# Turning softmax products and dense rows by transposing DMAs instead of TensorE, with layer 1's columns first

## The chip, the cores and the metric

The kernel runs on one core of a Trainium2 chip. The core has five engines with queues of their own: TensorE (PE, matmuls, with a separate lane PEld for loading weights), VectorE (DVE), ScalarE (ACT), GpSimd (POOL) and SyncE (SP, which computes nothing and issues DMAs). Sixteen DMA engines move data between HBM, SBUF and SBUF. The metric is the device time of one execution in microseconds (us).

## The reference

Four blocks follow each other: memory-augmented attention, a dense ReLU layer, and both again with the same weights. All tensors are bf16 outside.

```python
x = x + A(layernorm(x), mem0)      # layer 0
x = x + B(layernorm(x))
x = x + A(layernorm(x), mem0)      # layer 1
x = x + B(layernorm(x))            # x: [1, 2048, 512]

def A(x, mem):                     # 64 segments of 32 rows, 8 memory rows, 32 heads of 128
    for s in range(64):
        h = concat([mem, x[32*s:32*s+32]])          # 40 rows
        q, k, v = h @ Wq, h @ Wk, h @ Wv            # per head
        p = softmax(mask(q @ k.T * 128**-0.5))      # 40 x 40 per head
        o = (p @ v) @ Wo                            # 40 x 512
        mem, out[s] = o[:8], o[8:]                  # the memory goes into the next segment

def B(x): return relu(x @ w1) @ w2                  # 512 -> 1376 -> 512
```

The segments of one layer depend on each other through the eight memory rows: segment s + 1 cannot begin its queries, keys and values before segment s has its whole output projection.

## The kernel before

**Two layers at once.** A step k does segment k of layer 0 and segment k - 4 (`DELTA`) of layer 1 together. There are 68 steps; the first four and the last four have one layer alone. The two segments lie side by side as 80 columns (2 x `L`, L = 40) of a tile `HT` (two of them, used in turn), with the model dimension on the partitions: layer 0's 32 rows and 8 memory rows, then layer 1's 8 memory rows and 32 rows. All projections are matmuls with a 128 x 128 block of weights as the stationary operand and these 80 columns moving.

**A step.** `prep_x` (POOL) copies the next 32 normalised columns of each layer into `HT`. `step_values` makes the values of 64 columns (all that depend on the memory, and what else fits in 64); the other 16 rows of layer 0 are taken from values made ahead of time (`late_values`, `early_values`) and are brought from HBM by `place_values`, which also places the others: four DMAs V<-vw and two V<-vh per step on SP. Then five units follow (`UNITS`; units 0 to 2 have eight heads, units 3 and 4 four):

- `queries_keys`: Q and K of four heads at a time, 16 matmuls each, into one of five PSUM banks `work`; ACT or DVE copies them to `qT`, `kT`.
- `scores`: 40 x 40 products, half-width tiles (64 columns of the array), then the softmax in rows on DVE and ACT: mask (L1093), maximum (L1097), subtract (L1100), exp on ACT (L1104), sum (L1107), reciprocal (L1110), product (L1124) into `P`, with heads on partition halves and key columns along the row.
- still in `scores`: `P` is turned on TensorE, by a matmul with a unit matrix `ident` as the moving operand (`turn`, L665 through the helper `across`), into another `work` bank. Two copies (`keep`, L1147 on ACT or L1149 on DVE) multiply it by 1 or 0 by partition half (`half`), and so make a block-diagonal operand `PT` of two heads.
- `attend`: values times `PT` (L1166), copied to `OT`.

`project` multiplies `OT` by Wo for all heads into the bank `st`, and copies eight columns to the next `HT` (the memory) and 64 to `OX` (the rows). After every second step `finish_pair` takes two segments of each layer: it turns `OX` back into rows on TensorE (`turn`), adds x, and runs the dense layer: `layernorm` (statistics on DVE, the power on POOL), a turn of the normalised rows `xr` on TensorE with a copy to `xnM`, w1, ReLU, w2. Its rows for layer 0 are normalised again and turned into `xnB`, layer 1's input.

**Order.** The kernel is written out by hand ahead of the build. A planner (`Plan`) knows every operation with an assumed cost and its dependencies by tiles and keys, simulates six queues and gives each engine its order; `PLACE`, `AHEAD` and `RULE` are tables of due times that shift operations in it, and `PAIRED` names projections that may run as two half-width matmuls instead of one whole. The array loses time when it changes between whole (128 columns) and half-width (64) tiles, so the planner prefers to stay in a kind. Each engine then works through its own order and waits only on semaphores; the planner's costs decide the order and nothing else at run time. SP's order is fixed in the same way: a DMA whose data isn't ready holds up those behind it.

Buffers that matter here: five `work` banks, `qT` and `kT` of four tiles each, `es` two, `PT` three, and one `P` tile per unit pair (`Pt`), whose unused columns are zeroed once.

Of the kernel before, what the change touches and what calls it, by code (L numbers as in the profile page):

```python
# [10 lines left out]
ALU = mybir.AluOpType  # L11
# [19 lines left out]
RULE = (0.0676, 338.0438, 3554579.0286, 1242705613.0663)  # L31
PERIOD = 42.8582
PLACE = {
    ("attend.mmu0.0", 0): 608.991, ("attend.mmu0.0", 1): 157.899, ("attend.mmu0.0", 2): -380.976,
    ("attend.mmu0.0", 3): -849.744, ("attend.mmu0.0", 4): -420.014, ("attend.mmu0.0", 5): 379.888,
    ("attend.mmu0.0", 6): -935.369, ("attend.mmu1.0", 0): 724.653, ("attend.mmu1.0", 1): 735.673,
    ("attend.mmu1.0", 2): 83.429, ("attend.mmu1.0", 3): -335.179, ("attend.mmu1.0", 4): 3.094,
    ("attend.mmu1.0", 5): -935.256, ("attend.mmu1.0", 6): -23.81, ("attend.mmu2.0", 0): -313.198,
    ("attend.mmu2.0", 1): -1055.43, ("attend.mmu2.0", 2): 351.452, ("attend.mmu2.0", 3): -29.526,
    ("attend.mmu2.0", 4): -812.532, ("attend.mmu2.0", 5): 234.539, ("attend.mmu2.0", 6): -65.699,  # L40
    ("attend.mmu3.0", 0): 13.451, ("attend.mmu3.0", 1): 157.484, ("attend.mmu3.0", 2): 133.291,
    ("attend.mmu3.0", 3): -203.514, ("attend.mmu3.0", 4): 192.222, ("attend.mmu3.0", 5): -84.323,
    ("attend.mmu3.0", 6): -139.89, ("attend.mmu4.0", 0): -853.255, ("attend.mmu4.0", 1): -244.026,
    ("attend.mmu4.0", 2): -305.761, ("attend.mmu4.0", 3): -104.638, ("attend.mmu4.0", 4): -89.602,
    ("attend.mmu4.0", 5): -204.344, ("attend.mmu4.0", 6): 50.714, ("dense_layer.mm.0", 1): 822.894,
    ("dense_layer.mm.0", 3): 717.325, ("dense_layer.mm.0", 6): 792.485, ("dense_layer.mm.1", 1): -268.282,
    ("dense_layer.mm.1", 3): 157.778, ("dense_layer.mm.1", 6): -380.794, ("dense_layer.mm.2", 1): 376.492,
    ("dense_layer.mm.2", 3): 130.965, ("dense_layer.mm.2", 6): -212.381, ("dense_layer.mm.3", 1): -70.602,
    ("dense_layer.mm.3", 3): 419.403, ("dense_layer.mm.3", 6): -774.382, ("dense_layer.mm.4", 1): -244.79,
    ("dense_layer.mm.4", 3): 367.889, ("dense_layer.mm.4", 6): -182.649, ("dense_layer.mm.5", 1): 943.633,  # L50
    ("dense_layer.mm.5", 3): -26.387, ("dense_layer.mm.5", 6): 595.003, ("finish_pair.turn.0", 1): -125.119,
    ("finish_pair.turn.0", 3): -175.437, ("finish_pair.turn.0", 6): -732.778, ("g0", 2): -902.623,
    ("g1", 2): -345.827, ("g2", 2): 376.933, ("g3", 2): -860.996, ("g4", 2): 261.098, ("g5", 2): -902.521,
    ("g6", 2): 262.286, ("g7", 2): 447.122, ("late_values.mmv0.0", 0): 7.391, ("late_values.mmv1.0", 0): 723.22,
    ("late_values.mmv2.0", 0): -33.087, ("late_values.mmv3.0", 0): -918.158, ("late_values.mmv4.0", 0): 711.016,
    ("late_values.mmv5.0", 0): -29.506, ("late_values.mmv6.0", 0): -417.119, ("late_values.mmv7.0", 0): -388.807,
    ("layernorm.turn.0", 1): -11.687, ("layernorm.turn.0", 3): 291.45, ("layernorm.turn.0", 6): 74.607,
    ("layernorm.turn.1", 1): 932.83, ("layernorm.turn.1", 3): -23.815, ("layernorm.turnr.0", 0): 130.977,
    ("layernorm.turnr.1", 0): 22.148, ("prepare.turns.0", 2): 138.08, ("project.mm.0", 0): -28.38,
    ("project.mm.0", 1): -813.549, ("project.mm.0", 2): -352.721, ("project.mm.0", 3): 338.425,  # L60
    ("project.mm.0", 4): -85.099, ("project.mm.0", 5): 395.603, ("project.mm.0", 6): 258.346,
    ("project.mm.1", 0): 382.886, ("project.mm.1", 1): 332.847, ("project.mm.1", 2): -815.345,
    ("project.mm.1", 3): 420.621, ("project.mm.1", 4): -904.087, ("project.mm.1", 5): 539.837,
    ("project.mm.1", 6): 66.403, ("project.mm.2", 0): 332.311, ("project.mm.2", 1): -807.177,
    ("project.mm.2", 2): -643.677, ("project.mm.2", 3): 169.374, ("project.mm.2", 4): 38.108,
    ("project.mm.2", 5): 154.46, ("project.mm.2", 6): -123.487, ("project.mm.3", 0): -94.659,
    ("project.mm.3", 1): -2.385, ("project.mm.3", 2): -392.671, ("project.mm.3", 3): 755.857,
    ("project.mm.3", 4): 239.419, ("project.mm.3", 5): 449.254, ("project.mm.3", 6): 237.48,
    ("project.mm.4", 0): -28.331, ("project.mm.4", 1): -89.329, ("project.mm.4", 2): 233.897,
    ("project.mm.4", 3): -897.55, ("project.mm.4", 4): 4.166, ("project.mm.4", 5): -271.575,  # L70
    ("project.mm.4", 6): 68.861, ("queries_keys.mmu0.0", 0): -114.972, ("queries_keys.mmu0.0", 1): -803.223,
    ("queries_keys.mmu0.0", 2): 449.473, ("queries_keys.mmu0.0", 3): -814.936, ("queries_keys.mmu0.0", 4): 64.492,
    ("queries_keys.mmu0.0", 5): -247.66, ("queries_keys.mmu0.0", 6): -321.229, ("queries_keys.mmu0.1", 0): -246.448,
    ("queries_keys.mmu0.1", 1): -83.345, ("queries_keys.mmu0.1", 2): -93.12, ("queries_keys.mmu0.1", 3): -67.094,
    ("queries_keys.mmu0.1", 4): -882.377, ("queries_keys.mmu0.1", 5): -142.63, ("queries_keys.mmu0.1", 6): -836.169,
    ("queries_keys.mmu0.2", 0): -921.465, ("queries_keys.mmu0.2", 1): -331.089, ("queries_keys.mmu0.2", 2): -36.099,
    ("queries_keys.mmu0.2", 3): -153.588, ("queries_keys.mmu0.2", 4): 0.628, ("queries_keys.mmu0.2", 5): -845.834,
    ("queries_keys.mmu0.2", 6): -937.81, ("queries_keys.mmu0.3", 0): -75.904, ("queries_keys.mmu0.3", 1): -26.436,
    ("queries_keys.mmu0.3", 2): -78.722, ("queries_keys.mmu0.3", 3): -83.815, ("queries_keys.mmu0.3", 4): -874.602,
    ("queries_keys.mmu0.3", 5): -285.858, ("queries_keys.mmu0.3", 6): -288.873,  # L80
    ("queries_keys.mmu1.0", 0): -287.689, ("queries_keys.mmu1.0", 1): -807.17, ("queries_keys.mmu1.0", 2): 138.905,
    ("queries_keys.mmu1.0", 3): -775.344, ("queries_keys.mmu1.0", 4): 333.755, ("queries_keys.mmu1.0", 5): -69.094,
    ("queries_keys.mmu1.0", 6): -299.934, ("queries_keys.mmu1.1", 0): -894.335,
    ("queries_keys.mmu1.1", 1): -300.828, ("queries_keys.mmu1.1", 2): -195.096,
    ("queries_keys.mmu1.1", 3): -407.541, ("queries_keys.mmu1.1", 4): -99.416, ("queries_keys.mmu1.1", 5): -928.29,
    ("queries_keys.mmu1.1", 6): -1007.777, ("queries_keys.mmu1.2", 0): -397.855,
    ("queries_keys.mmu1.2", 1): -271.199, ("queries_keys.mmu1.2", 2): -95.574, ("queries_keys.mmu1.2", 3): -424.872,
    ("queries_keys.mmu1.2", 4): -828.244, ("queries_keys.mmu1.2", 5): -84.504, ("queries_keys.mmu1.2", 6): -365.113,
    ("queries_keys.mmu1.3", 0): -267.974, ("queries_keys.mmu1.3", 1): -319.862, ("queries_keys.mmu1.3", 2): 11.67,
    ("queries_keys.mmu1.3", 3): -410.531, ("queries_keys.mmu1.3", 4): 44.01, ("queries_keys.mmu1.3", 5): -391.768,  # L90
    ("queries_keys.mmu1.3", 6): -213.718, ("queries_keys.mmu2.0", 0): -65.556, ("queries_keys.mmu2.0", 1): -240.632,
    ("queries_keys.mmu2.0", 2): 64.693, ("queries_keys.mmu2.0", 3): 448.514, ("queries_keys.mmu2.0", 4): 417.76,
    ("queries_keys.mmu2.0", 5): 347.423, ("queries_keys.mmu2.0", 6): -104.214, ("queries_keys.mmu2.1", 0): -34.178,
    ("queries_keys.mmu2.1", 1): 23.812, ("queries_keys.mmu2.1", 2): -196.254, ("queries_keys.mmu2.1", 3): -337.37,
    ("queries_keys.mmu2.1", 4): 139.933, ("queries_keys.mmu2.1", 5): -92.169, ("queries_keys.mmu2.1", 6): 434.453,
    ("queries_keys.mmu2.2", 0): 129.446, ("queries_keys.mmu2.2", 1): 68.117, ("queries_keys.mmu2.2", 2): -78.718,
    ("queries_keys.mmu2.2", 3): -0.671, ("queries_keys.mmu2.2", 4): 460.034, ("queries_keys.mmu2.2", 5): 252.252,
# [103 lines left out]


def t_dve(n, rate=1):
    return 0.065 + 1.042e-3 * n / rate


PART, MASKED = {ACT: 0.13, DVE: 0.10}, {ACT: 0.11, DVE: 0.065}


def t_pool(n):  # L210
    return 0.06 + 2.2e-3 * n


# [204 lines left out]
def kernel(  # L418
# [529 lines left out]
    def htx(i, a):  # L948
        return [("HTx", i, a, (0, X1)[a])]
# [383 lines left out]
```

## Time and profile before

| | |
|---|---|
| times of the runs shown | 1629.60 and 1625.38 us, median 1627.49 |
| profiled execution: span from first to last instruction | 1624.3 us |
| mean granted TensorE clock | 0.998 |
| PE busy | 1584.0 us (98%), 43,678 matmuls recorded |
| PEld busy | 1378.5 us (85%) |
| ACT busy | 1095.1 us (67%) |
| DVE busy | 1031.9 us (64%) |
| POOL busy | 139.2 us (9%) |
| DMA | 63.37 MB, 39 GB/s in the mean, 372 GB/s in the first 40 us (weights) |

The profiled execution lists no time but its span; the times of the other executions stand 1 to 5 us above it. The page is read in this order: the busy shares tell which engine can be the bound; the chain that ended last tells where the end comes from; the waits tell what an engine stood still for, by the instruction that released it; the groups give count, busy time and mean duration of one kind of instruction by its line. Because matmuls are pipelined, the duration of one (200 ns) is longer than the distance from one to the next, and the line L665 is the helper `across`, shared by most matmuls: they are told apart by their tiles (`work<-ident,P` is the turn of P).

### The profile page before, as it was taken

What the parts mean: (1) busy time and instruction counts of PE and PEld (TensorE: products, weight loads), DVE (VectorE), ACT (ScalarE), POOL (GpSimd) and SP (SyncE); (2) the same over time, 40 slices, a digit from 0 to 9 for tenths busy, and PEclk for the clock granted to TensorE, in tenths of its full rate; (3) what the DMA queues carried; (4) which work ended last, traced back from release to release, by engine and by line L of the source; (5) the groups of instructions that cost most, each with busy time, mean ns of one, the idle gap of its engine ahead of it and who ended that gap; (6) DMA issues with size and microseconds to landing.
All of it is one profiled execution on the core that took longest, in us unless ns stands there. A gap on an engine that the chain in (4) does not pass through costs nothing.

```text
span 1624.3 us, 95837 instructions
## 1 busy us (share of the span) xinstructions
PE 1584.0 (98%) x43678; PEld 1378.5 (85%) x43746; DVE 1031.9 (64%) x2930; ACT 1095.1 (67%) x2813; POOL 139.2 (9%) x362
## 2 busy tenths in 40 slices
PE   7999999999999999999999999999999999999997
PEld 4688888888888888888888888888888888888886
DVE  4466756666665675676566567566656756665665
ACT  5567767766676776766677676667667766766664
POOL 4210000000000000100000000000000000000000
PEclk9999999999999999999999999999999999999999
DMA  9711001111100110111011011101101000000000
GB/s 372 264 23 33 19 22 29 23 27 34 34 21 21 29 25 25 35 28 26 22 30 25 26 35 28 25 22 26 27 25 28 23 21 19 17 20 19 19 6 6
DMA packets 42885, 63.37 MB, mean 39 GB/s; under 512 B 15400, under 2 KB 28816, under 8 KB 42480
## 3 DMA queue, kind: packets, MB, share of 16 engines
q1 hardware_dynamic: 35984, 35.88, 8.8%
q0 software_dynamic: 5328, 20.32, 3.3%
q8 instruction: 342, 5.60, 1.4%
q10 hardware_dynamic: 1168, 1.06, 0.2%
q14 instruction: 63, 0.52, 0.1%
HBM read 33.50 MB, written 11.93 MB: 28 GB/s over the span
## 4 chain that ended last, share of the span: by engine, by line
PE 94%; DVE 3%; issue 1%; ACT 1%; POOL 0%; DMA 0%; DVEq 0%; POOLq 0%; ACTq 0%
PE work L665 39%; PE st L665 19%; PE fill L998 15%; PE fill L665 12%; PE work L1166 4%; PE work L1082 3%; DVE es L1093 0%; DMA hT<-in_A_x_dram 0%; DVE mx L1097 0%; ACT HT L919 0%; PE fill L789 0%; DVE sm L1107 0%; DVE vw L921 0%; DVE PT L1149 0%; DVE es L1100 0%
## 5 line engine op out<-in xcount | busy, mean ns | idle before, releaser
L665 PE MATMUL work<-HT,Wq_sb 128*128 128x80 bf16 (+2 forms) x10208 | 369.3, 200 | 8.2 <-ACT HT L919 8.1
L665 PE MATMUL work<-HT,Wk_sb 128*128 128x80 bf16 (+2 forms) x10144 | 368.2, 200 | 2.4 <-issue 1.5
L665 PEld LDWEIGHTS <-Wq_sb 128*128 128x128 bf16 (+1 forms) x10208 | 330.4, 103 | 25.8 <-ACT HT L919 11.6
L665 PEld LDWEIGHTS <-Wk_sb 128*128 128x128 bf16 (+1 forms) x10144 | 333.4, 103 | 17.9 <-issue 3.5
L665 PE MATMUL st<-OT,Wo_sb 128*128 128x80 bf16 (+1 forms) x8704 | 339.7, 199 | 3.0 <-ACT OT L919 1.3
L665 PEld LDWEIGHTS <-Wo_sb 128*128 128x128 bf16 x8704 | 319.8, 99 | 11.7 <-issue 4.1
L919 ACT CAST qT<-work 128x320 bf16<-128x320 f32 (+1 forms) x484 | 197.7, 408 | 119.1 <-PE work L665 83.7
L998 PE MATMUL fill<-Wv_sb,HT 128*64 128x512 bf16 x2176 | 272.7, 381 | 0.5 <-POOL HT L938 0.5
L919 ACT CAST kT<-work 128x320 bf16<-128x320 f32 (+1 forms) x539 | 220.1, 409 | 58.5 <-PE work L665 18.7
L1147 ACT ACTIVATE PT<-work,half 128x320 bf16<-128x320 f32 (+2 forms) x448 | 200.6, 467 | 31.5 <-PE work L665 15.0
L919 ACT CAST vw<-fill 128x512 bf16<-128x512 f32 x227 | 132.8, 585 | 105.1 <-PE fill L998 103.0
L919 ACT CAST OT<-work 128x320 bf16<-128x320 f32 (+1 forms) x394 | 151.9, 413 | 76.4 <-PE work L1166 76.3
L1093 DVE TENSOR_TENSOR es<-work,maskb 128x320 f32<-128x320 f32 (+2 forms) x340 | 133.2, 402 | 60.3 <-PE work L1082 48.9
L998 PEld LDWEIGHTS <-HT 128*64 128x64 bf16 x2176 | 106.9, 110 | 70.5 <-issue 0.8
L884 DVE TENSOR_TENSOR xg<-xg,fill 128x512 f32<-128x512 f32 (+1 forms) x34 | 23.4, 688 | 185.9 <-PE fill L665 185.9
L1104 ACT ACTIVATE es<-es 128x320 f32<-128x320 f32 (+2 forms) x340 | 134.8, 406 | 7.4 <-DVE es L1100 3.5
L1100 DVE TENSOR_TENSOR es<-es,mx 128x320 f32<-128x320 f32 (+2 forms) x340 | 133.7, 404 | 2.6
L1097 DVE TENSOR_REDUCE mx<-es 128x8 f32<-128x320 f32 (+2 forms) x340 | 132.1, 399 | 3.6
L1124 DVE TENSOR_TENSOR P<-es,sm 128x320 bf16<-128x320 f32 (+2 forms) x338 | 131.1, 405 | 4.4
L1107 DVE TENSOR_REDUCE sm<-es 128x8 f32<-128x320 f32 (+2 forms) x340 | 130.9, 395 | 1.2 <-ACT es L1104 1.1
L1149 DVE TENSOR_SCALAR PT<-work,half 128x320 bf16<-128x320 f32 (+2 forms) x232 | 103.2, 454 | 26.6 <-PE work L665 24.3
L800 DVE TENSOR_TENSOR xg<-xg,fill 64x512 f32<-64x512 f32 x30 | 20.4, 681 | 140.5 <-PE fill L665 140.5
(98 smaller groups left out, 1801.7 us busy)
## 6 DMA issues: line engine op xcount, KB each, us to landing
V<-vw SPq DMA_DIRECT2D x240, 48.0 KB
V<-vh SPq DMA_DIRECT2D x120, 64.0 KB
Wq_sb<-in_A_Wq_dram POOLq DMA_DIRECT2D x2, 2048.0 KB, 21.0
Wk_sb<-in_A_Wk_dram POOLq DMA_DIRECT2D x2, 2048.0 KB, 25.4
Wo_sb<-in_A_Wo_dram POOLq DMA_DIRECT2D x2, 2048.0 KB, 37.1
vh<-vg SPq DMA_DIRECT2D x32, 128.0 KB
Wv_sb<-in_A_Wv_dram POOLq DMA_DIRECT2D x1, 2048.0 KB, 11.4
vh<-w_sb POOLq DMA_DIRECT2D x4, 512.0 KB, 5.3
```

Of the source, the lines that this page charges most:

```text
L665: nc.tensor.matmul(out_[u:v, :], lhsT=lhsT[:, u:v], rhs=rhs, start=start, stop=stop, tile_position=(0, u), **more)
L919: nc.scalar.copy(out=out_, in_=in_)
L998: nc.tensor.matmul(vp[64 * b:64 * b + 64, :], lhsT=cols(c4), rhs=Wv_sb[:, c4, n * 512:(n + 1) * 512], start=(c4 == 0), stop=(c4 == NC4 - 1 ...
L1093: nc.vector.tensor_tensor(out=flat(es[:, A]), in0=flat(sp[:, A]), op=ALU.add, in1=maskb[:, a_lo:a_hi, :].unsqueeze(2).to_broadcast([128, n ...
L1097: nc.vector.tensor_reduce(out=mx[:, As], in_=es3(), axis=AX.X, op=ALU.max)
L1100: nc.vector.tensor_tensor(out=es3(), in0=es3(), op=ALU.subtract, in1=mx[:, As].unsqueeze(2).to_broadcast([128, ns * na, L]))
L1104: nc.scalar.activation(out=es[:, A], in_=es[:, A], func=ACTF.Exp, scale=SCALE)
L1107: nc.vector.tensor_reduce(out=sm[:, As], in_=es3(), axis=AX.X, op=ALU.add)
L1124: (nc.gpsimd if eng == POOL else nc.vector).tensor_tensor(out=o, in0=flat(es[:, A]), op=ALU.mult, in1=sm[:, As].rearrange("p (a s) -> p a ...
L1147: nc.scalar.activation(out=o, in_=i, func=ACTF.Copy, scale=half[:, b:b + 1])
L1149: nc.vector.tensor_scalar_mul(out=o, in0=i, scalar1=half[:, b:b + 1])
L1166: nc.tensor.matmul(o[u:u + cols, :, a, :], lhsT=V[:, p, e0 + u:e0 + u + cols], rhs=PT[:, a, 2 * i + h2, :, :], start=True, stop=True, tile ...
```

## The change

1. **P is turned by DMA.** The product L1124 now writes `P` in blocks of 256 columns: 64 of zeros, head A's keys, head B's keys, 64 of zeros, each in 64 columns. Cut in blocks of 128 and transposed, that is already the block-diagonal operand. One transposing DMA per unit, issued from SP, turns rows 0 to 111 of all blocks into `PT`. The turn on TensorE, its `work` bank, and the two mask copies are gone. `P` is a ring of two tiles, zeroed once.
2. **OX and the normalised dense rows are turned by DMA** too (`finish_pair.turn`, `layernorm.turn_far`), into SBUF; the turns on TensorE and the copies from PSUM are gone. The turns of layer 0's input (`halved`) stay on TensorE.
3. **Layer 1's columns come first** in `HT`, `OT`, `OX` and the rows of the dense layer; layer 0's come second. `HT` has L + 64 columns.
4. `qT` and `kT` have three tiles each instead of four and are taken in order.
5. The tables `RULE`, `PLACE`, `PAIRED` and `AHEAD` have new numbers (left out below); the planner is given 0.5 + 0.2 per block of 128 columns as SP's cost and 2.6 as the delay of a transposing DMA (`XBAR`).

```diff
-PART, MASKED = {ACT: 0.13, DVE: 0.10}, {ACT: 0.11, DVE: 0.065}
+PART = {ACT: 0.13, DVE: 0.10}
+XBAR = 0.5, 0.2, 2.6
...
-    HTs = [sb(f"HT{i}", [128, NC4, 2 * L]) for i in range(2)]
-    PL = 256 + LK[1]
-    Pt = [sb(f"P{p}", [128, 2 * PL]) for p in range(4)]
+    HTs = [sb(f"HT{i}", [128, NC4, L + 64]) for i in range(2)]
+    p_P = ring("P", 2, [128, 8 * 128])
...
-    p_qT, p_kT = ring("qT", 4, [128, 4, 2 * L]), ring("kT", 4, [128, 4, 2 * L])
+    p_qT, p_kT = ring("qT", 3, [128, 4, 2 * L], BF, True), ring("kT", 3, [128, 4, 2 * L], BF, True)
...
-    p_PT = ring("PT", 3, [128, 2, 4, 2, L])
+    p_PT = ring("PT", 3, [128, 8, 112])
...
+        def turn_far():
+            nc.sync.dma_start_transpose(out=xnT[:, :, to:to + n], in_=xn[R, :])
...
+        if not halved:
+            plan.op(SP, XBAR[0] + XBAR[1] * NC4 * n / 128, turn_far, r=[xn], w=[xnT], lag=XBAR[2])
+            return xnT
...
-        x, ox, y = x_tiles[j], ox_tiles[j], b_fill.buf()
+        x, ox, y = x_tiles[j], ox_tiles[j], p_xr.buf()
...
-        def turn(cols):
-            T = slice(0, 128 if 1 in act else PR)
-            for c4 in range(NC4):
-                across(cols, y[:, c4 * 128:(c4 + 1) * 128], ox[:, c4, T], ident[:])
+        def turn():
+            nc.sync.dma_start_transpose(out=y[:, :].rearrange("t (c d) -> t c d", c=NC4),
+                                        in_=ox[:, :, :].rearrange("p c t -> p (c t)"))
...
-        plan.op(PE, 0.23, turn, r=[ox, "ident"], w=[y], tile=EITHER, count=4)
+        plan.op(SP, XBAR[0] + XBAR[1] * NC4, turn, r=[ox], w=[y], lag=XBAR[2])
...
-            values(lambda c4: HTs[i][:, c4, HS:2 * L], lambda p: vw[:, p, :], lambda p: [("vw", p)], deps)
+            values(lambda c4: HTs[i][:, c4, 0:64], lambda p: vw[:, p, :], lambda p: [("vw", p)], deps)
...
-        sp, mx, es, sm, tp = b_work.buf(), p_mx.buf(), p_es.buf(), p_sm.buf(), b_work.buf()
-        P = Pt[p]
+        sp, mx, es, sm = b_work.buf(), p_mx.buf(), p_es.buf(), p_sm.buf()
+        P = p_P.buf()
...
+        NT = 2 * nx * na
+
         def mul(eng):
-            o = P[:, :].rearrange("p (a c) -> p a c", a=2)[:, a_lo:a_hi, 128 * xs[0]:128 * xs[-1] + 128]
-            o = o.rearrange("p a (s k) -> p a s k", k=64)[:, :, :, 0:L]
+            o = P[:, 0:128 * NT].rearrange("p (z e k) -> p z e k", e=4, k=64)[:, :, 1:3, 0:L]
...
-        def turn(cols):
-            rhs = ident[:, :].rearrange("p (g q) -> p g q", g=2)[:, :, 0:L]
-            for a in range(a_lo, a_hi):
-                for i, x in enumerate(xs):
-                    z = nx * a + i
-                    c0 = 256 * a + 128 * x
-                    across(cols, tp[:, z * 2 * L:(z + 1) * 2 * L], P[:, c0:c0 + 128], rhs)
-
         PT = p_PT.buf()
-        plan.op(PE, nx * na * 0.0358, turn, r=[*[("P", p, b, x) for b in range(2) for x in xs], "ident"], w=[tp, PT],
-                tile=EITHER, count=nx * na)
-
-        for b in range(2):
-            def keep(eng, b=b):
-                o = PT[:, a_lo:a_hi, 0:2 * nx, b, :]
-                i = tp[:, A].rearrange("p (a g q) -> p a g q", g=2 * nx, q=L)
-                if eng == ACT:
-                    nc.scalar.activation(out=o, in_=i, func=ACTF.Copy, scale=half[:, b:b + 1])
-                else:
-                    nc.vector.tensor_scalar_mul(out=o, in0=i, scalar1=half[:, b:b + 1])
-
-            copy_op(n, keep, r=[tp, PT, "half"], w=[(PT, b)], more=MASKED)
+
+        def turn():
+            nc.sync.dma_start_transpose(out=PT[:, 0:NT, :], in_=P[0:112, 0:128 * NT])
+
+        plan.op(SP, XBAR[0] + XBAR[1] * 2 * na * nx, turn, r=[P], w=[PT], lag=XBAR[2])
...
                             nc.tensor.matmul(o[u:u + cols, :, a, :], lhsT=V[:, p, e0 + u:e0 + u + cols],
-                                             rhs=PT[:, a, 2 * i + h2, :, :], start=True, stop=True, tile_position=(0, u))
+                                             rhs=PT[:, 2 * (nx * (a - a_lo) + i):2 * (nx * (a - a_lo) + i) + 2, 64 * h2:64 * h2 + L], start=True, stop=True, tile_position=(0, u))
```

## The prediction

> **What bounds the kernel now.** I read first the page's busy line and its chain that ended last, then what the PE waited for once the weights are in (80 to 1600 us).
>
> ```profile
> span 1624.3 us, 95837 instructions
> ...
> PE 1584.0 (98%) x43678; PEld 1378.5 (85%) x43746; DVE 1031.9 (64%) x2930; ACT 1095.1 (67%) x2813; POOL 139.2 (9%) x362
> ...
> PE 94%; DVE 3%; issue 1%; ACT 1%; POOL 0%; DMA 0%; DVEq 0%; POOLq 0%; ACTq 0%
> ```
>
> ```profile
> PE work L665 <- ACT HT L919: 8.7, 29, 0.3
> PE st L665 <- ACT OT L919: 1.3, 7, 0.4
> ```
>
> The PE is the bound without a gap: all its waits in 1520 us come to about 13 us, and 8.7 of them are the one place per pair of steps where the next step's columns wait for the projection. Whatever leaves the PE's own queue is a gain, unless a new wait takes its place. ACT (67%) and DVE (64%) have a third of their time free, SP's queue and the DMA engines more.
>
> The second view is the groups of instructions:
>
> ```profile
> L665 PE MATMUL work<-HT,Wq_sb 128*128 128x80 bf16 (+2 forms) x10208 | 369.3, 200 | 8.2 <-ACT HT L919 8.1
> L665 PE MATMUL work<-ident,P 128*64 128x80 bf16 (+1 forms) x1546 | 87.5, 202 | 2.6 <-DVE P L1124 0.9 <-ACT OT L919 0.5 <-DVE sm L1107 0.5
> L665 PE MATMUL fill<-ident,xr 128*64 128x128 bf16 (+3 forms) x496 | 28.9, 212 | 13.9 <-DVE xr L716 13.9
> L665 PE MATMUL fill<-ident,OX 128*128 128x128 bf16 (+1 forms) x136 | 13.3, 220 | 0.4 <-ACT OX L919 0.4
> ```
>
> A matmul of 80 columns lasts 200 ns but the PE starts one every 369.3 / 10208 = 36 ns; busy time of short groups is therefore an upper bound (87.5 for the P turns), count times pace a lower one (1024 turns, halves counted as one, by 36 ns: 37 us). From the records in order of time, taking each from its start to the next matmul's start, the P turns hold the PE for 52.8 us, the OX turns for 11.3, and the xr turns that go for about 15. I use these.
>
> **Part by part, against the span of 1624.3** (the two times shown, 1625.4 and 1629.6, have a median 3.2 us above it; I add that at the end).
>
> 1. *Turns leave the PE*: 52.8 + 11.3 + 15 = 79 us. This is on the path.
>
> 2. *The PE's order is rewritten.* Read from the two instruction orders: the products for Q, K, V, scores, attend and Wo stay the same number of columns; what differs is that the array changes between whole and half-width tiles 505 times instead of 303. Each such change costs 0.107 us in the records (mean step minus pace over the 303). 202 x 0.107 = +22 us. So the PE's own work falls to 1624.3 - 79 + 22 = **1567 us**.
>
> 3. *The mask copies L1147 (ACT, 200.6 us, 448 of them) and L1149 (DVE, 103.2 us, 232) go*, and the casts after the dense turns. Neither engine is the bound, so by themselves they give nothing, 0; they clear the softmax chain for point 4. If ACT had been the cover of something, the waits above would show it; at most the 13 us of PE waits could go too. About 40 products P move to POOL, which is 9% busy: 0.
>
> 4. *What is late next.* P must now go DVE -> SP -> DMA -> PE instead of DVE -> PE -> ACT/DVE -> PE. The last unit of a step shows the old path best (PE, DVE and their tiles in order of time; start, duration):
>
> ```profile
> 820.53 0.26 PE L1082 MATMUL work<-kT,qT 128*40 128x40 bf16 x8
> ...
> 820.98 0.32 DVE L1093 TENSOR_TENSOR es<-work,maskb 128x160 f32<-128x160 f32 x1
> ...
> 823.39 0.33 DVE L1124 TENSOR_TENSOR P<-es,sm 128x160 bf16<-128x160 f32 x1
> ...
> 823.83 0.24 PE L665 MATMUL work<-ident,P 128*128 128x80 bf16 x2
> ...
> 825.91 0.20 PE L1166 MATMUL work<-PT,V 128*128 128x80 bf16 x1
> ```
>
> Scores end at 820.79, P is there at 823.72 (2.9 us), turned and copied by 824.78, and used at 825.91: 5.1 us, 1.1 to spare. In the new order I counted the PE's work, at its pace, between a unit's scores and its attend. In even steps all units have 8 us or more. In 22 of the 30 full odd steps the last two units have 4.2 and 5.0 us, in 8 (those with most work for later values between) 5.0 and 5.8. Their P exists after 2.9 us. So the transpose has 1.3 to 2.1 us, and the two queue behind each other on SP.
>
> No row shows a transposing DMA. The nearest are plain DMAs on the same queue:
>
> ```profile
> L1024 SPq DMA_DIRECT2D V<-vw x32: 717/722/1230, 717.1 to 890.3; - x32
> ...
> L842 SPq DMA_DIRECT2D xh<-xnE x8: 540/549/959, 112.4 to 978.1; - x8
> ```
>
> V<-vw (within SBUF, 48 KB) holds SP 0.72 us and its semaphore is full 2.1 us after the issue began (788.02 to 790.14). xh<-xnE (128 KB in 1024 pieces of 128 bytes, the size and grain closest to a small P of 114 KB) holds SP 0.54 and its last piece is down 2.0 to 2.7 us after. Dearest: vh<-w_sb, 512 KB, 5.3 us; the longest SP issue of V<-vh, 1.83. I take 0.72 to issue and 2.4 to land, nearest to xnE. Lean odd step: 2.9 + 2.4 - 4.2 = 1.1 us of stall, and the second unit (2.9 + 0.72 + 2.4 - 5.1 = 0.9) hides in it; rich: 0.3. 22 x 1.1 + 8 x 0.3 = **+27 us**. The ends: 0 if it lands in 1.3 us; at 1.83 and 5.3, 22 x 4.9 + 8 x 4.1 = 141, and even steps (2.9 + 1.83 + 5.3 - 8.2 = 1.8) 54 more: +195.
>
> The eight steps with one layer alone have 3.4 to 5 us there and little else to do; I add 1 us each, **+8**. The last dense layer does two transposes in series, each 2.4 for a turn and copy of some 0.9: **+3**.
>
> 5. *SP's queue.* A pair of steps (47.4 us) gets 13 transposes beside the placing of values (8 x 0.72 + 4 x 0.36) and some 1.3 us of loads, 8.5 in all. At 0.72 each that is 18 us; behind a transpose that waits for P stand V's copies, which are needed only a step later. Cost 0, until 13 of them average over 3.0 us.
>
> 6. *DMA engines.* 2048 blocks of 112 x 128 and the dense rows are about 70 MB, more than the 63 of now. At xnE's 13 ns per 128 bytes that is 27% of 16 engines on top of 10%; at 48 ns per 1024 bytes 13%. The PE's instructions come over the same engines:
>
> ```profile
> 40.00:80.00 40.00, 37.10 (x930) 27.69 (x928) 17.73 (x70) 22.29 (x67) 8.23 (x18) 1.00 0.79 273
> 80.00:700.00 620.00, 613.29 (x17135) 538.06 (x17157) 407.25 (x1138) 428.18 (x1089) 49.77 (x133) 1.00 0.11 27
> ```
>
> (busy PE, PEld, DVE, ACT, POOL, clock, DMA share, GB/s). At a share of 0.79 the PE loses 2.2 us of 40 to "issue", at 0.11 practically nothing. I take 0, and keep 5.5% of 1500 us, 84, as the other end.
>
> The new columns' order (layer 1 first) moves no work: 64 columns for values before and after. 0.
>
> Sum: 1567 + 27 + 8 + 3 = 1605 span, + 3 = **1608 us**.
>
> A page speaks against the change. The Trainium skill, "VectorE: DVE Perf Modes", section "The three transpose paths", has 390 ns for a 128 x 128 turn on TensorE and 1309 ns by DMA, and its rules send such turns to TensorE if PSUM will do; 32 blocks a step one after another would be 42 us, nearly twice the step, some 2.7 ms in all. No row here has that price. "DMA: Bandwidth & Descriptors", section "Why a DMA increments its semaphore by 16 and not by 1" (its table on the sequencer's decode time), gives for earlier generations 631 cycles a transpose and 262,144 for 8192 tiles, 32 a tile: at the 1.2 GHz of "Trainium Kernel Development and Optimization", section "NeuronCore Architecture", I estimate 1.27 us for a small P. With V<-vw's 1.37 from issue's end to landing the stalls would be 22 x 1.7 + 8 x 0.9 = 45 and the sum 1626.
>
> **Rivals.**
> *The wait is hidden (1578 to 1592):* without mask copies on ACT and DVE the softmax is faster than 2.9 us: 820.98 to 823.71 contains 0.9 us of DVE waiting for ACT's copies and other work. Then point 4's 27 shrinks to 0 to 12. For: both engines lose 300 us. Against: the transpose still has only some 2 us.
> *SP and the crossbar are slow (1677):* at the tail of the odd steps; at twice a plain copy (1.44 to issue, 4.2 to land) the second unit needs 2.9 + 1.44 + 4.2 - 5.1 = 3.4: 22 x 3.4 + 8 x 2.6 = 96, 1567 + 96 + 11 + 3. It decides from issue plus landing of 4.8 us, where the stalls pass 78 and the time 2%. For: a transpose of 28 to 56 tiles is more to issue than a copy. Against: V<-vw and xnE both land below 2.7.
> *Instructions come late (1640 to 1690):* point 6 at half or all of 84. Against: the engines' share should be near 0.4, not 0.79.
> That the turns don't leave the PE is excluded: no matmul of ident with P or OX is left in the order, and SP has 440 transposes.
>
> **Chances.** Forecast (stalls of 15 to 60 us, 1595 to 1645) 0.42; hidden 0.30; slow transposes 0.20; late instructions 0.08. A measurement tells about 2% from no change, 1595 to 1660. Faster: the hidden case and the forecast's lower edge, 0.32. Slower: slow transposes and most of late instructions, 0.26. Same 0.42. Range: from 1567 (nothing stalls and the 13 us of waits go) to 1690; above it I leave the saturated SP queue.
>
> **What would show it.** P turns gone and ACT near 890 us busy: point 3. PE waits on "DMA PT" near 27 us, once per pair of steps, before the last attends: point 4; near zero is the hidden case, over 80 the slow one. SP's rows give issue times: 0.7 expected, over 2 wrong. "issue" waits of the PE in mid-run would show the late instructions. I am wrong on the low side if the PE's order has fewer half-width changes' worth of loss than 22 us, on the high side if a transpose holds SP for more than 3 us.

## The result, and the profile after

The changed kernel takes **1787.13 us** (1785.53 and 1788.73) against 1627.49: a ratio of 1.098, 95% interval 1.096 to 1.100. It is slower by 160 us, 97 us above the range of the prediction. First the page of the changed kernel: span, busy times, chain that ended last.

```profile
span 1787.0 us, 95396 instructions
...
PE 1624.0 (91%) x43334; PEld 1363.2 (76%) x43334; DVE 1012.1 (57%) x2608; ACT 927.7 (52%) x2344; POOL 177.5 (10%) x404
...
PE 77%; DMA 13%; ACT 4%; DVE 3%; issue 1%; POOL 1%; SPq 0%; POOLq 0%; DVEq 0%; ACTq 0%
```

PE is still the busiest, but a fifth of the chain now runs through DMA, ACT and DVE; before, PE had 94% of it. ACT lost 167 us of work, and the time did not fall for it. What PE waited for from 80 to 1770 us (engine and line, what it waited for, us in all, times, longest):

```profile
PE st L655 <- ACT OT L911: 66.1, 148, 0.9
PE work L1143 <- DMA PT<-P: 32.7, 44, 1.5
PE work L655 <- ACT HT L911: 19.0, 63, 0.3
```

Before, the same three places had 1.3, nothing and 8.7. The largest wait is not for the transposing DMA. It is for a copy on ACT that both kernels have: products with V (L1143) are copied to `OT` (L911), and Wo reads `OT`. The end of an odd step shows how that comes about (all engines in order of time; start, duration, [idle before <- releaser]):

```profile
902.09 0.38 PE L1074 MATMUL work<-kT,qT 128*40 128x40 bf16 x16
...
905.02 0.32 DVE L1117 TENSOR_TENSOR P<-es,sm 128x160 bf16<-128x160 f32 x1
...
905.46 3.93 SPq L1126 DMA_TRANSPOSE PT<-P  x2
905.46 0.33 DVE L1117 TENSOR_TENSOR P<-es,sm 128x160 bf16<-128x160 f32 x1
...
906.80 1.31 PE L655 MATMUL st<-OT,Wo_sb 128*128 128x80 bf16 x32 [0.37 <-ACT OT L911]
908.84 0.20 PE L1143 MATMUL work<-PT,vw 128*128 128x80 bf16 x1 [0.74 <-DMA PT<-P]
...
909.66 0.73 PE L655 MATMUL st<-OT,Wo_sb 128*128 128x80 bf16 x16 [0.51 <-ACT OT L911]
910.58 0.20 PE L1143 MATMUL work<-PT,vw 128*128 128x80 bf16 x1 [0.19 <-DMA PT<-P]
...
911.40 0.73 PE L655 MATMUL st<-OT,Wo_sb 128*128 128x80 bf16 x16 [0.52 <-ACT OT L911]
...
912.44 0.75 PE L655 MATMUL work<-HT,Wq_sb 128*128 128x80 bf16 x16 [0.30 <-ACT HT L911]
```

The last scores end at 902.47, both P are there by 905.79, the two turns follow each other on SP until 909.39, and PE does products, waits for a copy to `OT`, does Wo, and so on, with nothing else left in its queue: 2.6 us idle in the last 6. The last attend comes 8.1 us after the scores; in the kernel before it came after 4.8 on average.

From the records I took the time from one copy of the memory columns to the next, which is a step, and the time by which each matmul starts later than its size's pace allows (only amounts over 0.15 us, by what ended the wait). "Slow clock" is the rest of such delay while the granted clock stands at half. The rows of waits and clock are for the whole run.

| us | before | after |
|---|---|---|
| mean of steps 6 to 62, even | 25.4 | 26.5 |
| mean of steps 7 to 63, odd | 22.3 | 25.4 |
| steps 0 to 5, from PE's first matmul | 151.6 | 174.9 |
| last four steps, to PE's last matmul | 79.4 | 94.0 |
| late at products with V, for PT | - | 50 |
| late at Wo, for OT's copies | 8 | 96 |
| late at the next step, for HT's copy | 14 | 30 |
| slow clock | 1 | 24 |
| change of tile, whole to half-width or back | 30 | 39 |

An odd step loses 4.5 us to waits, where it lost 0.6. An even step, which has the dense layer to fill its queue, loses 0.8. The profile also shows what a transposing DMA costs SP (duration in ns: min, median, max; first and last start):

```profile
L1126 SPq DMA_TRANSPOSE PT<-P x340: 1165/1242/2723, 36.1 to 1765.9; - x170
```

From the start of its issue to its last semaphore write (those of the kernel after 80 us that the records show whole, some 430) it takes 2.26 us at best, 3.25 in the mean, 4.3 at the ninth tenth, 5.2 at most.

### The profile page after: what moved, and what is told of

Same layout as the page of the kernel before. It is cut to its first block, busy times and chain, and to the rows that moved or that the text cites. A ratio compares the mean times of both kernels' runs of the same rounds, so it can differ in the third digit from the quotient of the medians.

```text
span 1787.0 us, 95396 instructions
## 1 busy us (share of the span) xinstructions
PE 1624.0 (91%) x43334; PEld 1363.2 (76%) x43334; DVE 1012.1 (57%) x2608; ACT 927.7 (52%) x2344; POOL 177.5 (10%) x404
## 4 chain that ended last, share of the span: by engine, by line
PE 77%; DMA 13%; ACT 4%; DVE 3%; issue 1%; POOL 1%; SPq 0%; POOLq 0%; DVEq 0%; ACTq 0%
PE work L655 34%; PE fill L990 13%; PE st L655 13%; DMA PT<-P 11%; PE fill L655 9%; PE work L1074 4%; PE work L1143 4%; ACT OT L911 2%; DMA xnM<-xr 1%; ACT HT L911 1%; DVE es L1085 1%; ACT es L1096 1%; DVE es L1092 1%; DVE mx L1089 1%; DMA V<-vw 0%
## 5 line engine op out<-in xcount | busy, mean ns | idle before, releaser
L655 PE MATMUL st<-OT,Wo_sb 128*128 128x80 bf16 (+2 forms) x10592 | 363.6, 200 | 68.1 <-ACT OT L911 66.1
L655 PEld LDWEIGHTS <-Wo_sb 128*128 128x128 bf16 (+1 forms) x10592 | 341.6, 104 | 95.6 <-issue 81.9
L655 PE MATMUL work<-HT,Wq_sb 128*128 128x80 bf16 (+2 forms) x10144 | 381.1, 201 | 18.1 <-ACT HT L911 17.9
L911 ACT CAST OT<-work 128x320 bf16<-128x320 f32 (+1 forms) x463 | 180.0, 414 | 294.9 <-PE work L1143 294.7
L911 ACT CAST kT<-work 128x320 bf16<-128x320 f32 (+1 forms) x538 | 222.0, 413 | 79.1 <-PE work L655 48.3
L911 ACT CAST qT<-work 128x320 bf16<-128x320 f32 (+1 forms) x476 | 194.6, 409 | 87.7 <-PE work L655 57.1
L911 ACT CAST vw<-fill 128x512 bf16<-128x512 f32 x228 | 133.6, 586 | 134.0 <-PE fill L990 132.2
L1092 DVE TENSOR_TENSOR es<-es,mx 128x320 f32<-128x320 f32 (+2 forms) x340 | 150.7, 443 | 11.6
L876 DVE TENSOR_TENSOR xg<-xg,xr 128x512 f32<-128x512 f32 (+1 forms) x34 | 23.5, 691 | 227.6 <-DMA xr<-OX 227.6
L1143 PE MATMUL work<-PT,vw 128*64 128x80 bf16 (+1 forms) x1408 | 116.0, 201 | 31.0 <-DMA PT<-P 29.2
L1117 DVE TENSOR_TENSOR P<-es,sm 128x320 bf16<-128x320 f32 (+2 forms) x298 | 121.0, 406 | 35.8 <-DMA PT<-P 27.5
L1143 PE MATMUL work<-PT,V 128*64 128x80 bf16 (+1 forms) x1412 | 114.6, 202 | 13.9 <-DMA PT<-P 12.5
L1143 PEld LDWEIGHTS <-V 128*64 128x64 bf16 (+1 forms) x1412 | 83.5, 107 | 52.5 <-issue 43.8
```

The costliest lines, as they stand in the source:

```text
L655: nc.tensor.matmul(out_[u:v, :], lhsT=lhsT[:, u:v], rhs=rhs, start=start, stop=stop, tile_position=(0, u), **more)
L876: nc.vector.tensor_tensor(out=x[R, :], in0=x[R, :], in1=y[R, :], op=ALU.add)
L911: nc.scalar.copy(out=out_, in_=in_)
L1092: nc.vector.tensor_tensor(out=es3(), in0=es3(), op=ALU.subtract, in1=mx[:, As].unsqueeze(2).to_broadcast([128, ns * na, L]))
L1117: (nc.gpsimd if eng == POOL else nc.vector).tensor_tensor(out=o, in0=es[:, A].rearrange("p (z b k) -> p z b k", b=2, k=L), op=ALU.mult, in ...
L1143: nc.tensor.matmul(o[u:u + cols, :, a, :], lhsT=V[:, p, e0 + u:e0 + u + cols], rhs=PT[:, 2 * (nx * (a - a_lo) + i):2 * (nx * (a - a_lo) + ...
```

## The experiments

Line numbers shift in the kernels whose tables are written one entry to a line. "Late" is counted as in the table above; waits given without a window are those of the whole run. `e1`, `e4`, `e5`, `e8` and `e13` were executed once, the other experiments four times, with 3 to 11 us between the lowest and the highest, so a few us between single runs mean nothing.

**Is it the wait for PT, the order, or the traffic?** `e1_constant` changes one operand:

```diff
-   rhs=PT[:, 2 * (nx * (a - a_lo) + i):... + 2, 64 * h2:64 * h2 + L]
+   rhs=ident[:, 0:2 * L].rearrange("p (b q) -> p b q", b=2)
```

> The changed kernel with its order untouched; every product with V reads the unit matrix in place of PT, so nothing waits for a transposing DMA any more, while all 440 transposing DMAs are still issued and still write PT (the softmax therefore no longer reaches the output). Theory A, the queue is bare: TensorE's order ends each odd step with product, copy to OT, Wo, four times in a row and nothing between, so the waits for OT (66 us) stay, and only the 42 us of waits for PT and a part of the 46 us of lower clock go: 1710 to 1750 us. Theory B, the path's delay alone: with PT free at once nearly everything comes back, 1660 us or less. Theory C, the traffic: only the waits for PT go and the small losses stay, about 1740 us.

Measured: 1730.48 us. Its waits for OT from 80 to 1700 us:

```profile
PE st L655 <- ACT OT L911: 63.6, 142, 0.9
```

Theory B falls in the form in which it was put: without a single wait for PT the kernel is still 103 us slower than before. The waits for OT stand as they were, as theory A said. The 57 us between this run and the changed kernel are the waits for PT and the slow clock behind them (24 us in the changed kernel, 5 here).

`e13_no_p_turns` takes the same kernel and leaves the 340 DMAs out (`turn` of P is empty):

```diff
-            nc.sync.dma_start_transpose(out=PT[:, 0:NT, :], in_=P[0:112, 0:128 * NT])
+            pass
```

> e1_constant (the changed kernel's order, the unit matrix in place of PT) and the 340 transposing DMAs of P are not issued at all. e1 had 1730 us. If what is left there is the order (waits for OT of 95 us in the records): 1710 to 1735 us. If it is the DMAs' side effects (SP's queue, 58 MB of 256-byte packets, VectorE waiting for a free P tile): 1640 to 1690 us.

Measured: 1711.71 us. SP's queue, the traffic and VectorE's waits for a free tile of P are worth 19 us. The order alone, without any DMA of P, is slower than the kernel before by 84:

```profile
PE st L655 <- ACT OT L911: 65.1, 145, 1.1
```

`e5_one_block` goes the other way and keeps every wait, with an eighth or a quarter of the data:

```diff
-   nc.sync.dma_start_transpose(out=PT[:, 0:NT, :], in_=P[0:112, 0:128 * NT])
+   nc.sync.dma_start_transpose(out=PT[:, 0:1, :], in_=P[0:112, 0:128])
```

> The changed kernel with its order untouched; every transposing DMA of P turns only the first of its four or eight blocks of 128 columns, so these DMAs move a quarter or an eighth of the data while the number of issues and all waits stay (the other blocks of PT hold a constant, so the output is not the reference's). Theory A and theory B: issue stays near 1.2 us, the landing comes up to 0.6 us earlier for each of the last units: 1745 to 1780 us. Theory C, the traffic of 256-byte packets: 1700 us or less.

Measured: 1756.82 us. The mean from issue to last write falls from 3.25 to 2.86 us, and the time by 30. Theory C (traffic) falls with this and e13.

**Which part of the change?** Two kernels keep the order of the kernel before on every engine and replace turns one for one. `e2_dense_only` issues a transposing DMA where the turns of OX and xr stood:

```diff
+                nc.sync.dma_start_transpose(out=xnT[:, :, to:to + n], in_=xn[R, :])
...
-            for c4 in range(NC4):
-                across(cols, y[:, c4 * 128:(c4 + 1) * 128], ox[:, c4, T], ident[:])
+            nc.sync.dma_start_transpose(out=yt[:, :].rearrange("t (c d) -> t c d", c=NC4),
+                                        in_=ox[:, :, :].rearrange("p c t -> p (c t)"))
```

> The kernel before with its order kept on every engine; only OX and the normalised dense rows (xr) are turned by transposing DMAs, P stays on TensorE. 26 us of turns leave TensorE. If the dense rows have the slack that the order of before gives them: 1600 to 1615 us. If each of them is late by the 2.4 us of a transposing DMA against the 0.9 us of a turn and a copy, three per pair of steps: 34 times up to 4.5 us more and 1625 to 1700 us.

Measured: 1654.92 us, ratio 1.017 (1.015 to 1.018), inside the second case. Most even steps gain 0.4 us; but five lose 3.0 to 4.3, since the next step's columns come late through xnB, and each of these five stalls of 2.2 to 3.5 us is followed by 3.4 us at half clock. Another 8.7 us are one wait for xnM at the end. The stalls at the columns:

```profile
PE work L668 <- POOL HT L948: 18.5, 8, 3.5
```

`e4_p_only` does it for P alone, in the changed kernel's layout, and so also has two tiles of P where the kernel before has four:

```diff
-    Pt = [sb(f"P{p}", [128, 2 * PL]) for p in range(4)]
+    Pt = [sb(f"P{p}", [128, 8 * 128]) for p in range(2)]
...
-                    across(cols, tp[:, z * 2 * L:(z + 1) * 2 * L], P[:, c0:c0 + 128], rhs)
+            nc.sync.dma_start_transpose(out=PT[:, 0:NT, :], in_=P[0:112, 0:128 * NT])
```

> The kernel before with its order kept on every engine; only P is turned by transposing DMAs into block-diagonal operands, issued where TensorE's turn stood, and the mask copies are gone; the dense rows stay on TensorE. Theory A, the changed kernel's order is the larger part of the loss: 53 us of turns go, the last two units of an odd step wait 1 to 2 us for PT (29 times), even steps 0.3 us: 1620 to 1690 us. Theory B, the path's delay is it, whatever the order: 1740 us or more. Theory C, the traffic: 1700 us or more with few waits for PT.

Measured: 1960.32 us. My theory A missed by 270 us, and the time lies in theory B's range. PE waits for the turns (from 80 to 1700 us), and VectorE waits for a turn to have read one of the two tiles of P (whole run):

```profile
PE work L1156 <- DMA PT<-P: 210.8, 150, 3.4
```

```profile
DVE P L1124 <- DMA PT<-P: 206.3, 120, 4.0
```

The old order leaves a turn the time that a matmul and a copy need, in every unit and in even steps too. How much of the 332 us over the kernel before comes from the delay and how much from having two tiles of P fewer, this run does not tell. But the changed kernel, with two tiles as well, is 173 us faster, so its order is not simply bad: it had made room. That this room is what it pays for in OT waits is tested below.

**Can another order have both?** `e6_replanned` has the operations of the changed kernel, planned with a shorter delay and newly searched tables:

```diff
-XBAR = 0.5, 0.2, 2.6
+XBAR = 1.4, 0.0, 1.2
```

> The changed kernel with the same operations and the same transposing DMAs, in another order: the planner is told a transposing DMA's measured cost (1.4 us on SP, 1.2 us from there to the data, where it had 1.3 to 2.1 and 2.6), and the tables of due times are searched anew under it. Theory A, the loss is the order that was written for the change: the waits for OT at the end of odd steps fall from 66 us to under 20, those for PT stay under 40, the clock stays near 0.99: 1620 to 1670 us. Theory B, the path is too long for this recurrence in any order: 1720 us or more, with the waits moved and not gone.

Measured: 1801.53 us, 1.107 (1.104 to 1.110). The waits have moved:

```profile
PE work L1427 <- DMA PT<-P: 121.7, 107, 8.1
...
PE st L939 <- ACT OT L1195: 9.9, 29, 0.4
```

Theory A falls here too, and the time lies in theory B's range: the waits for OT are nearly gone as A said (9.9 us against 66.1), and those for PT have grown instead (121.7 against 41.8 in the whole of the changed kernel). 2.6 us from issue to data was the delay of a quiet turn and not the mean. `e8_replanned_constant` puts the unit matrix in this order, with the edit of `e1_constant`:

> The order of e6_replanned on every engine, and every product with V reads the unit matrix in place of PT, as in e1_constant, so that no product waits for a transposing DMA (the softmap product does not reach the output). If the length of the path is what this order loses, the 142 us that PE falls behind at PT and most of the slow clock go: 1615 to 1665 us, 70 us or more below the order of the changed kernel under the same cut (1730). If the traffic or the order itself is the loss, 1720 us or more.

Measured: 1716.40 us, just short of the upper case, and so not what I expected of the path alone. In this order the turns hold PE by another way, the two tiles of P: VectorE waits for a turn to have read one, and a copy to OT stands behind it in VectorE's queue. All 26 of PE's waits for a copy on VectorE had such a wait just before them there.

```profile
DVE P L1401 <- DMA PT<-P: 89.5, 58, 6.2
```

```profile
PE st L939 <- DVE OT L1197: 26.9, 26, 2.8
```

`e9_replanned_mean` is planned with the mean of the records, 3.35 us:

```diff
-XBAR = 0.5, 0.2, 2.6
+XBAR = 1.45, 0.0, 1.9
```

> The changed kernel's operations in a third order: the planner is told the mean that the records of e6 show from the start of a transposing DMA's issue to its last semaphore write, 3.35 us (1.45 on SP and 1.9 after), in place of 2.6 (e6) or 3.9 to 4.7 (the changed kernel), and the tables are searched under it. If the path's delay must be either waited for or planned around, this order lies between: 1690 to 1765 us, below both 1787 and 1801, with waits for PT of 40 to 90 us and waits for OT of 10 to 50. If something else than this delay holds the kernel, it stays at 1780 or more.

Measured: 1783.43 us, 1.094 (1.093 to 1.096). The time missed its range and lies in the one for another cause than the delay; the waits lie where they were expected, and both are there:

```profile
PE work L1416 <- DMA PT<-P: 75.4, 78, 7.6
PE st L928 <- ACT OT L1184: 47.0, 105, 0.5
```

The 78 turns that PE waited for had landed 4.47 us after their issue began, in the mean; 90% of them took longer than the 3.35 planned, of all turns of P 43%. So an order that is right for the mean loses at the late ones. Three orders, planned for 2.6, 3.35 and 3.9 to 4.7 us, give 1801, 1783 and 1787. Between them the waits change places: the more delay an order plans for, the less PE waits for PT (121.7, 75.4 and 41.8 us) and the more for ACT's copies to OT (9.9, 47.0 and 66.1).

**What if the turn took no time?** `e12_free_turn` drops the turn of P from the changed kernel: the products read P itself. P has three tiles here, in place of two of P and three of `PT`, and the tables are searched anew.

```diff
-    p_P = ring("P", 2, [128, 8 * 128])
+    p_P = ring("P", 3, [128, 8 * 128])
...
-        plan.op(SP, XBAR[0] + XBAR[1] * 2 * na * nx, turn, r=[P], w=[PT], lag=XBAR[2])
-        return PT
+        return P
```

> The changed kernel without any transposing DMA of P: the products with V read P as it stands, unturned (so the output is not the reference's), and wait for the product that writes it; P has three tiles in place of two of P and three of PT. The dense rows stay on transposing DMAs. The tables are searched for it. It stands for a turn of P that costs nothing and takes no time. If the delay of the turn is what the changed kernel loses, waited for or planned around: 1565 to 1610 us, near the 1567 that the prediction gave as TensorE's own work. If the loss lies in the rest of the change (columns, smaller rings, dense rows): 1650 us or more.

Measured: **1568.68 us**, 0.964 (0.962 to 0.966). The page and PE's largest wait in mid-run:

```profile
PE 1523.4 (97%) x43961; PEld 1315.2 (84%) x44052; DVE 972.6 (62%) x2705; ACT 918.2 (59%) x2287; POOL 140.7 (9%) x365
```

```profile
PE work L932 <- ACT HT L1188: 6.6, 22, 0.3
```

PE hardly waits for OT any more (0.2 us in all); odd steps take 21.1 us and even ones 24.6, and the last products come 3.2 us after the last scores. This settles which part of the change costs the time: with an order that suits them, the dense rows by DMA, the columns' order and the smaller rings of `qT` and `kT` stand 59 us below the kernel before, of which the turns of P that are gone make 37. The 218 us between this kernel and the changed one come with the turn of P by DMA and its two tiles of P: 143 us in the order that makes room for it (1711.7 - 1568.7), 19 in the DMAs' side effects, 57 in waits for PT with slow clock.

**Where does a DMA turn fit?** `e7_last_units_on_pe` and `e10_tail_pe_mean` turn P of the last two units of each step on TensorE, from the same blocks of P (four matmuls and one copy), and are planned with 2.6 and 3.35 us for the other turns:

```diff
+        if nx == 1:
+            tp = b_work.buf()
+            ...
+            plan.op(PE, NT * 0.0358, turn, r=[P, "ident"], w=[tp, PT], tile=EITHER, count=NT)
+            copy_op(NT * 2 * L, keep, r=[tp], w=[PT])
+            return PT
```

> As the run before it, but the last two units of every step (four heads each) have P turned on TensorE again, from the same blocks, with one copy by ACT or DVE; units 0 to 2 and the dense rows stay on transposing DMAs; the tables are searched for this kernel. It costs TensorE 68 times 8 matmuls of 36 ns, 20 us. Theory A and the tail as its place: the last attends no longer wait for a DMA, nearly no waits for PT or OT at the end of odd steps: 1595 to 1640 us. If the three early units' DMAs and the dense rows are late too, 1650 us or more.

> As e7_last_units_on_pe (P of the last two units of a step turned on TensorE), with the planner told 3.35 us: the three early units of a step and the dense rows have room for it, the last two need none: 1640 to 1700 us, waits for PT under 40 us. If the early units' turns are late as well, 1710 us or more.

Measured: 1716.96 us (1.055, 1.053 to 1.057) and 1693.81 us (1.040, 1.038 to 1.041). The first missed its lower range and lies in the one for early units that are late as well. The second lies in its range, but waited longer for PT than the 40 us expected. Against `e9`, which was planned with the same delay, it gains 90 us, and odd steps go from 25.4 to 23.4 us: of the 4.3 us by which an odd step of `e9` is longer than one of `e12`, the last two units' turns make 2. Of the other 2.3, 0.9 are waits for the early units' turns; what the rest is, no run shows:

```profile
PE work L1457 <- DMA PT<-P: 53.7, 50, 8.0
```

`e11_dense_replanned` leaves all of P on TensorE and has only the dense rows by DMA, planned with 3.65 us:

```diff
-XBAR = 0.5, 0.2, 2.6
+XBAR = 1.45, 0.0, 2.2
...
-            nc.sync.dma_start_transpose(out=PT[:, 0:NT, :], in_=P[0:112, 0:128 * NT])
+                    across(cols, tp[:, z * 2 * L:(z + 1) * 2 * L], P[:, c0:c0 + 128], rhs)
```

> The kernel before with P on TensorE; only OX and the normalised dense rows go by transposing DMA, and the tables are searched for it with 3.65 us for such a DMA. The turns of the dense rows are some 18 us at TensorE's pace, and e2_dense_only lost them to six stalls of 2 to 4 us with slow clock behind them. With room planned for them: 1605 to 1640 us. If the dense rows' chain is too long for one pair of steps in any order: 1655 us or more.

Measured: 1627.51 us against 1629.56 for the kernel before on that chip, 0.9985 (0.9971 to 0.9999). It is the fastest version that computes the whole, but by 2 us, 0.15%, which is hardly a gain. Even steps gain 0.5 us, but the first six and the last four steps lose 12 together. At the end, where nothing else is left to do, one wait for xnM is 8.4 us long; the kernel before waits 3.8 there.

## Why the prediction was wrong

- *What bounds the kernel* was right: PE without a gap, and its own work is the floor. For "PE's own work" 1567 was only 11 us low, but that is luck: two errors nearly cancelled. The turns that leave are 55 us at PE's pace and not 79 (36.7 for P, 7.4 for OX, 10.9 for xr), since counting each from its start to the next matmul's start took in changes of tile that stayed; and the changes of tile cost 9 more and not 22: 1624 - 55 + 9 = 1578. That e12's span is 1565.6 does not confirm the figure; its order has 387 changes of tile in the whole run, the changed kernel's 569.
- *The mask copies give nothing*: right. ACT fell to 928 us (890 forecast), and the time did not fall for it.
- *The size of the new path failed first.* I took 0.72 us to issue and 2.4 to land, the nearest copies' figures. Measured: 1.41 to issue and 3.25 to the last write, 2.26 at best. By the prediction's own formula that gives a lean odd step 2.9 + 3.3 - 4.2 = 2.0 us at the first unit and 2.9 + 1.4 + 3.3 - 5.0 = 2.6 at the second, a rich one 1.8: 22 x 2.6 + 8 x 1.8 = 72 us in place of 27, and a sum of 1653. So the wrong size explains a quarter of the miss of 179 us.
- *The step that failed worst is point 4, "What is late next".* I priced one wait, for PT, as if the 4.2 and 5.0 us of PE work behind the last scores ran without waits. They did not: PE reaches the last units with only their own products and Wo left, so each copy to OT is waited for, four times in an odd step, 88 us more than before. Waits for HT (16 more) and the slow clock (23 more) come on top. The wait that I did price, 27 + 8 us, came to 50. What is more than forecast in these four (88, 16, 23 and 15 us) and the 11 us of the first point make 153 of the 179; the rest is not assigned.
- *"PE's own work" and the order.* I read the new order for how many changes of tile it has, not for what stands behind each copy. e13 shows what that left out: without any DMA of P this order costs 143 us more than e12's, and PE is 97 us late at Wo for OT's copies, where in e12 it is late by 0.2.
- *SP's queue*: cost 0 was nearly right; queue, traffic and tiles together are 19 us.
- *Late instructions* was the wrong way round: PE did not wait more for its instructions, but the late turns had instruction loads beside them (below).
- *The rival of a slow SP and crossbar* (1.44 to issue, 4.2 to land, 1677) was nearest, with an issue as it was measured (1.41), and 110 us short for the same reason: it priced waits for PT alone.
- The Trainium skill's rule that speaks against the change ("VectorE: DVE Perf Modes", "Rules for kernel authors": TensorE for a 128 x 128 turn if PSUM will do) points the right way. The 1309 ns per 128 x 128 block of "The three transpose paths" are not what was paid: a turn of eight blocks of 112 x 128 issued in 1.24 us and had landed in 2.9 when nothing was in its way.
- From the skill's table of decode times ("DMA: Bandwidth & Descriptors", "Why a DMA increments its semaphore by 16 and not by 1") I estimated 1.27 us of issue for a small P, and 1.19 were measured. That is luck: the table's 631 cycles are for a transpose from HBM, and the same working gives an estimate of 2.02 us for a large P, and 1.24 were measured.

What stays open: whether some order hides this path. Three orders did not; that is not a proof. No run has the turns by DMA with a third tile of P either. In the changed kernel's order VectorE waits 28 us for a turn to have read a tile, and by e13 that costs at most 19 us there, queue and traffic included; but the planner laid out that order for two tiles, and in e4, e6 and e8 these waits are longer (206, 61 and 90 us). That the late turns are what defeats the order planned for the mean is read from the records of e9, and no run had turns without that spread.

## What to carry to other kernels

In a recurrence whose engine is full, the delay of a path counts and not its engine time: 37 us of turns of P were bought off, 340 times, with a path some 2 us longer in the mean and 4 at most (3.3 and 5.2 us against the 1.1 of a turn and a copy), and the kernel lost 160 us, 218 against a turn that takes no time. Before moving work to a longer path, follow the engine's queue to the end of the step and ask of each copy what the engine does meanwhile; when the last independent work is gone, every link of the chain is paid. Plan a DMA on a critical chain by its late landings and not by its quietest one.

## What the runs showed of the hardware

**Late transposing DMAs had an instruction load beside them.** The instruction queue moved 339 packets of 16 KB in the changed kernel, each 1.14 us long in the mean. Of the 116 transposing issues longer than 1.5 us, 115 had such a packet in flight, of the 304 shorter than 1.3 us 31%. Where a load was running 0.8 us after an issue began (113 times), the issue ended 0.40 to 0.55 us after the load did in eight cases of ten. Example: the turn issued at 905.46 met a load from 905.22 to 906.58, held SP 2.19 us and landed after 3.35; the next, issued at 908.17 with no load near, took 1.21 and 2.37. After 80 us, turns of P without a load between issue and landing landed after 2.5 us in the mean (57), the others after 3.5 (268). This mixes sizes, but in full steps it holds for each: 2.39 against 3.23 us with four blocks, 2.94 against 3.68 with eight. Every turn above 3.35 us had a load; but a turn that takes longer also meets more loads. Plain copies V<-vw took 2.13 us without and 2.73 with one. The Trainium skill says that the cost of crossing a boundary of 16 KiB is "one DMA tail-bump, mostly hidden" ("Runtime: NRT & Kernel Launch", "Instruction fetch mechanics"); by these records other DMAs pay for it. That the loads cause the delay is read from the records and not shown: no run varied them.

**Half a clock after 2.1 us of idling within 3.4 us, in pieces.** The granted clock drops to one half in stretches of 3.4 us or multiples of it. I cut five kernels (the changed one, e1, e2, e4, e5) from 80 us on into windows of that length, in step with the drops, and counted in those at full clock the time in which no matmul streamed (0.42 ns for each moving column, from the 217 ns that the PE takes from one matmul of 512 columns to the next). Of 2,221 windows with less than 0.6 of the time idle none was followed by a low one, of 61 with 0.6 to 0.7 thirty, and all 45 above 0.7. In the changed kernel the window from 647.5 us was idle for 0.64 of its time in pieces of at most 0.72 us, and a low one followed. In e2, from 100 to 1600 us, the five stalls of 2.2 to 3.5 us were each followed by a low stretch, the four of 1.1 to 2.0 us by none. The Trainium skill has the same window of 3.4 us, but asks for an idle window ("TensorE: Matmul & The Clock Gate", "Part 1: The HAM clock gate"); measured, 2.1 us of idling in pieces are enough. By an estimate, half of one such stretch, a stall of 3 us can cost up to 1.7 more behind it.
